# Row maxima sent into lasting score tiles by four small DMAs a step instead of four VectorE scalings, with another order of TensorE's slots

## The chip, the cores and the metric

The kernel runs on one core of a Trainium2 chip. The metric is the device time of one execution in microseconds (us); the median of several runs is compared. The engines are called as the profile calls them: PE is TensorE (PEld its weight loads), DVE is VectorE, ACT is ScalarE, POOL is GpSimd, SP is SyncE, which here only issues DMAs.

## The reference

One transformer block over 2048 tokens of width 1024, with a conditioning vector c that shifts, scales and gates both halves. The attention half treats the tokens as four segments of 512; each of 32 heads (of width 32) takes a causal softmax inside the segment and adds, by a gate of its own, what a linear-attention memory M of all earlier segments gives. The FFN half is gated by GELU. Cut to what matters:

```python
h = _layernorm(x) * (1 + ca) + sa
q, k, v = heads(h @ wq), heads(h @ wk), heads(h @ wv)   # 32 heads, 4 segments of 512
for s in range(4):
    logits = q[s] @ k[s].T * Dh**-0.5 + mask             # causal inside the segment
    a_dot = softmax(logits) @ v[s]
    pq = phi(q[s])                                       # phi(t) = t + 1 if t > 0 else exp(t)
    a_mem = (pq @ M) / (pq @ z + 1e-6)
    o[s] = g * a_mem + (1 - g) * a_dot
    M, z = M + phi(k[s]).T @ v[s], z + phi(k[s]).sum(0)
x = x + ga * (concat(o) @ wo)
h = _layernorm(x) * (1 + cb) + sb
x = x + gb * ((gelu(h @ w_gate) * (h @ w_up)) @ w_down)
```

## The kernel before, in words

**Two parts.** The attention fills about the first 1000 us, the output projection and the FFN the rest. The change touches only the attention. Products keep more than one pass's precision: each operand is split into a high and a low part, and `mm` (L318) issues three matmuls for each of the eight pieces of the contraction (hi x hi, hi x lo, lo x hi): 24 matmuls of 512 columns for each of q, k and v of a step.

**Steps.** `steps` (L1489) lists 32 attention steps. A step is a group g of four heads (j = 0 to 3) in one segment s; segments 0 and 1 go through all eight groups, then segments 2 and 3. Iteration n of the loop runs the scores (`scores`) and the memory (`memory`, `sums`) of step n, the values (`values`) of step n - 1, and the k, v and q products (`kv_part`, `q_part`) of step n + 1.

**Scores twice.** `scores` computes S = q k (L658, row i of 128 queries, head j) to find each row's maximum and sum: DVE adds the mask and takes the negated maximum mm (`sj`, L660), ACT takes the exponential and its row sum ll (L662). `values` computes the transposed scores T = k q again (L722, chunk kc of 128 keys, head j), so that exp(T) (`pt`, L724) can go straight into the product with v (O, L731), after POOL has cut it at the diagonal (L725). The maximum must be subtracted inside the T matmul. For that the tiles ks and qs have 128 rows: rows 0 to 95 hold three pieces of k and q (sent there by DMA, L350 and L378), and rows 96 to 127 hold, in ks, a one-hot pattern of the head (`selj`, written once, L461), and in qs, minus the maximum. Which of these 32 rows carries the maximum of which query block and head is fixed by the pattern `eye`.

**How the maxima reach qs.** The 16 maxima of a partition are split in hi and lo (`mt`, L668 and L669), transposed by DVE in four pieces of 32x32 (`tt`, L673), and then written four times, once for each block i of 128 queries, by a scaling of all 32 rows (L675): row r of tt times `seli[r, i]`, which is one where the row belongs to block i and zero elsewhere. So the rows of other blocks become zero in the same instruction. qs is a fresh tile for each step, two buffers of tag "qs" in turn.

**What frees what.** PSUM has two buffers "mm" (v, k and q products in turn), five "s" (S, T, the transposes vT, kT, R, Y, and the memory's sums) and one "o" (O). A v product's buffer is freed by ACT's copy `vr` (L325); a k product's by `kh`, `kl` and `kn` (L340, L341, L345); a q product's by `qh` (L367), `ql` (L368), and from segment 1 on by `eq` and, last, `pq` (L376).

**Order.** PE's order is written by hand. In each iteration of the loop the string ORDER (ORDER0 in the first) is read letter by letter, and each letter takes the next piece of one generator: V values, S scores, A sums, M memory, K kv_part, Q q_part, N the layernorm of the segments to come, side loads at odd positions. One K piece is two of the eight pieces of a product, 6 matmuls; four K pieces make v, four make k (the transposes vT in the middle of the second), the ninth sends k. In the first eight steps the letter N also brings transposes of the norm. DVE, ACT, POOL and SP are ordered by a scheduler in the loop; in `start()` they too run in the order of the code.

**The start.** `start()` (L415 on) does the layernorm of segments 0 and 1, the conditioning products and step 0's q, k and v. The norm of segment 1 is the generator `norm`; each `next(norm)` does one tile of 128 tokens: statistics on DVE, the inverse root as a power on POOL (L197, `rsa`), a product on DVE (`mra`, L480), the scaling on DVE and ACT (`rx`, L484 and L486).

**Late loads.** `load_late` (L828) puts half of wo into four tiles that the attention no longer uses: two fresh ones of tag "qs" and the two ks tiles.

Of the kernel before, what the change touches and what calls it, by code (L numbers as in the profile page):

```python
# [12 lines left out]
F32R = mybir.dt.float32r  # L13
AF = mybir.ActivationFunctionType
ALU = mybir.AluOpType
# [4 lines left out]
P = 128  # L20
# [9 lines left out]
L = 512  # L30
# [6 lines left out]
def block_kernel(ctx: ExitStack, tc: tile.TileContext, x, c, wmod, wms, wq, wk, wv, wo, beta, wg, wu, wd, out):  # L37
    nc = tc.nc
    f32 = lambda ap: ap.bitcast(F32)
# [45 lines left out]
    def t2(name, tag, bufs=1, dt=F32, shape=(P, L)):  # L85
        return (p1 if tag in ("qs", "row") else pa).tile(list(shape), dt, name=name, tag=tag, bufs=bufs)

    def cs(shape, name, dt=F32, **kw):
        return const.tile(shape, dt, name=name, **kw)
# [10 lines left out]
    ones = cs([P, P], "ones")  # L100
    ident = cs([P, P], "ident")
    mask = pa.tile([P, L], F32, name="mask")
    sel4 = cs([P, 4], "sel4")
    blk = pa.tile([P, P], F32, name="blk")
    selj = cs([P, 4], "selj")
    seli = cs([P, 4], "seli")
    mhalf = cs([P, 4], "mhalf")
    bb = cs([P, H], "bb")
    gall = cs([P, H], "gall")
# [181 lines left out]


    hT, W, Mst, ST, SC, PK = {}, {}, {}, {}, {}, {}
    ks_t = []
    for n in range(2):
        k = p1.tile([P, 4, L], F32R, name=f"ks{n}")
        ks_t.append(k)
# [66 lines left out]
    def q_out(n, s, nm, ps):  # L364
        qh = t2("qh" + nm, "sp", bufs=4, dt=F32R)
        ql = t2("ql" + nm, "sp" if n else "sj", bufs=4 if n else 3, dt=F32R)
        nc.scalar.activation(qh, ps, AF.Copy, scale=SCALE)  # L367
        nc.vector.scalar_tensor_tensor(ql, ps, SCALE, f32(qh), op0=ALU.mult, op1=ALU.subtract)  # L368
        qs = t2("qs" + nm, "qs", bufs=2, dt=F32R, shape=(P, 4, L))
        pq = None  # L370
        if s > 0:
            e = tmp_tile("eq" + nm)
            nc.scalar.activation(e, ps, AF.Exp)
            nc.vector.tensor_scalar_min(e, e, 1.0)
            pq = t2("pq" + nm, "pq", bufs=2)
            nc.vector.scalar_tensor_tensor(pq, ps, 0.0, e, op0=ALU.max, op1=ALU.add)  # L376
        for qd, srct in ((0, qh), (1, ql), (2, qh)):
            nc.sync.dma_start(f32(qs[32 * qd:32 * qd + 32]), f32(srct))  # L378
        state(n)[0], state(n)[3] = qs, pq
# [35 lines left out]
    def start():  # L415
# [20 lines left out]
        def select(dst, src, **kw):  # L436
            nc.gpsimd.affine_select(dst, src, **kw)

        nc.vector.memset(ones, 1.0)
        eye = tmp_tile("eye")[:, :32].rearrange("p (j i l) -> p j i l", j=4, i=4)  # L440
        select(eye, ones[:, :32].rearrange("p (j i l) -> p j i l", j=4, i=4), pattern=[[-8, 4], [-2, 4], [-1, 2]],
               compare_op=ALU.is_equal, fill=0.0, base=-96, channel_multiplier=1)
        select(ident, ones, pattern=[[-1, P]], compare_op=ALU.is_equal, fill=0.0, base=0, channel_multiplier=1)
        pick = tmp_tile("pick")[:, :P].rearrange("p (j d) -> p j d", d=DH)
# [7 lines left out]

        nc.vector.memset(mhalf, -0.5)
        nc.vector.tensor_reduce(selj, eye.rearrange("p j i l -> p j (i l)"), axis=AX.X, op=ALU.add)
        nc.vector.tensor_copy(seli, eye[:, 0, :, 0])
        for j in range(4):
            for part in range(2):
                if j or part:
                    nc.vector.tensor_add(seli, seli, eye[:, j, :, part])
        for k in ks_t:  # L460
            nc.scalar.activation(k[96:128], selj[96:128].unsqueeze(2).to_broadcast([32, 4, L]), AF.Copy)  # L461
            if k is ks_t[0]:
# [152 lines left out]
        low(7)  # L615
        products(6, 7)
        next(norm)
        kk = k_out(0, nm, ps[2])
        k_send(0, *kk)
        q_out(0, 0, nm, ps[0])  # L620
# [26 lines left out]
    def scores(n, g, s):  # L647
# [5 lines left out]
        for i in range(4):  # L653
            nk = max(256, (i + 1) * P)
            nv = (i + 1) * P
            for j in range(4):
                ps = s_ps(f"S{nm}_{j}{i}")
                nc.tensor.matmul(ps[:, :nk], qs[:96, j, i * P:(i + 1) * P], ks[:96, j, :nk], start=True, stop=True)  # L658
                sj = t2(f"sj{nm}_{j}{i}", "sj", bufs=3)
                nc.vector.tensor_tensor_reduce(out=sj[:, :nv], in0=ps[:, :nv], in1=mask[:, L - nv:], scale=-1.0,  # L660
                                               scalar=3.4e38, op0=ALU.add, op1=ALU.min, accum_out=mm[:, j, i:i + 1])
                nc.scalar.activation(sj[:, :nv], sj[:, :nv], AF.Exp, bias=mm[:, j, i:i + 1], scale=-1.0,  # L662
                                     accum_out=ll[:, i, j:j + 1])
            if i < 3:
                yield
# [6 lines left out]
        for a in range(4):  # L672
            nc.vector.transpose(tt[96:128, 32 * a:32 * a + 32], mtf[32 * a:32 * a + 32])  # L673
        for i in range(4):
            nc.vector.tensor_scalar(qs[96:128, :, i * P:(i + 1) * P], tt[96:128].unsqueeze(1).to_broadcast([32, 4, P]),  # L675
                                    seli[96:128, i:i + 1], None, op0=ALU.mult)

        rc = t2("rc" + nm, "rc", bufs=2, shape=(P, 4, 4))
        nc.vector.reciprocal(rc, ll)
# [147 lines left out]

    def load_late():  # L828
        rs = [None] * 5
        for k in range(5):  # L830
            if k < 4:
                rs[k] = fetch(wo[1, k], f"o1_{k}")
            if k > 0:
                w = t2(f"wo1_{k}", "qs", bufs=2, dt=F32R, shape=(P, 4, L)) if k < 3 else ks_t[k - 3]
                wot[1].append(split_w(gated(rs[k - 1], 1), w.rearrange("p (a b) t -> p a (b t)", a=2)))
            yield

# [648 lines left out]


    steps = [(hf, g, s) for hf in range(2) for g in range(G) for s in (2 * hf, 2 * hf + 1)]
    ORDER = "K N K K V K V N K K V V K N V K S Q S V V Q S Q A S K M Q V V"  # L1489
    ORDER0 = "N N N N N N N N K K K K S K S K S K A S K Q Q Q K M Q"  # L1490
    none = iter(())
    todo = []
# [115 lines left out]
```

## Time and profile before

| what | value |
|---|---|
| median of 3 runs | 2776.38 us (2775.57 to 2776.82) |
| the profiled execution's own time | 2777.42 us |
| its span | 2775.6 us |
| mean granted TensorE clock | 0.999 |
| busy share of PE, DVE, ACT, POOL | 98%, 63%, 46%, 20% |
| the 128 scalings into qs (L675) on DVE | 479 ns at least, 481 median, 1035 at most, from 76.8 to 978.4 us |

A row of a timeline gives the start in us, the duration in us (of a group of like instructions, from the first's start to the last's end), the engine, the line, the operation, "out<-in" by the program's names, the tile's shape and the count; in brackets stands how long the engine was idle ahead of it and which instruction it waited for. A row of the waits gives who waited, on whom, the sum in us, the number of times and the longest. A row of the windows gives a stretch of the span, its length, the busy time of PE, PEld, DVE, ACT and POOL in it, the granted clock, and the share and rate of the DMAs.

### The profile page before, as it was taken

To read this page: it belongs to the slowest core of one execution; us is meant where nothing else is said; L and a number is where in the kernel's file an instruction comes from. 1 tells how busy PE (TensorE), PEld (TensorE's weight loads), DVE (VectorE), ACT (ScalarE), POOL (GpSimd) and SP (SyncE) were. 2 spreads that over 40 slices of the span, in tenths; PEclk is the share of its full clock that TensorE was granted. 3 is DMA by queue.
4 is the path that set the end of the run, shared out by engine and by line. 5 is a ranking of instruction groups with operands and counts; after the bars stand their busy time and mean duration, and the time that the engine had idled before them with its cause. 6 is when DMAs were issued, how large, how long until landed. Compare 5 with 4: busy or idle time off the path is not lost.

```text
span 2775.6 us, 38577 instructions
## 1 busy us (share of the span) xinstructions
PE 2729.4 (98%) x13336; PEld 2206.0 (79%) x13336; DVE 1760.7 (63%) x3719; ACT 1287.3 (46%) x2855; POOL 542.0 (20%) x988
## 2 busy tenths in 40 slices
PE   7999999999999999999999999999999999999999
PEld 5777777777777777888888887888888888888887
DVE  7665657767565844777776768667778754434543
ACT  6788767677676735234343324233223243332220
POOL 1333333333332531100000002000000002012442
PEclk9999999999999999999999999999999999999999
DMA  7666656665555648655655644334567595544652
GB/s 258 125 142 152 146 114 129 150 135 126 114 111 96 156 164 252 194 208 208 218 202 195 239 169 167 123 145 143 190 239 254 213 314 177 181 138 156 206 188 80
DMA packets 229604, 480.18 MB, mean 173 GB/s; under 512 B 17440, under 2 KB 92192, under 8 KB 229408
## 3 DMA queue, kind: packets, MB, share of 16 engines
q1 hardware_dynamic: 229408, 477.72, 57.1%
q8 instruction: 105, 1.72, 0.3%
q14 instruction: 91, 0.75, 0.1%
HBM read 300.96 MB, written 126.35 MB: 154 GB/s over the span
## 4 chain that ended last, share of the span: by engine, by line
PE 86%; DVE 6%; issue 2%; ACT 2%; DMA 1%; POOL 1%; SPq 0%; DVEq 0%; ACTq 0%; POOLq 0%
PE f L1286 36%; PE d L1452 19%; PE k L318 6%; PE q L318 5%; PE y L790 5%; PE v L318 3%; PE S L658 3%; PE O L731 3%; PE T L722 3%; DVE qs L675 1%; PE M L638 1%; DVE sj L660 1%; PE R L745 1%; PE num L696 1%; PE vT L334 0%
## 5 line engine op out<-in xcount | busy, mean ns | idle before, releaser
L1286 PE MATMUL f<-A,B 128*128 128x512 f32 x4704 | 1073.2, 390 | 4.4 <-DVE c L1251 2.7
L1286 PEld LDWEIGHTS f<-A,B 128*128 128x128 f32 x4704 | 881.3, 188 | 189.7 <-issue 2.3
L1452 PE MATMUL d<-wb,ah 128*128 128x512 f32 x2352 | 534.3, 389 | 0.2 <-DVE wb L1337 0.2
L1452 PEld LDWEIGHTS d<-wb,ah 128*128 128x128 f32 x2352 | 441.3, 188 | 92.9 <-DVE wb L1337 0.8
L660 DVE CUSTOM_DVE_ANT_0 sj<-S,mask 128x384 f32<-128x384 f32 (+3 forms) x512 | 227.8, 487 | 183.2 <-PE S L658 174.5
L662 ACT ACTIVATE sj<-sj,mm 128x384 f32<-128x384 f32 (+3 forms) x512 | 282.3, 556 | 28.2 <-DVE mm L660 26.0
L724 ACT ACTIVATE pt<-T 128x256 f32<-128x256 f32 (+3 forms) x512 | 184.9, 457 | 119.0 <-PE T L722 113.4
L1337 DVE TENSOR_TENSOR ah<-ar,ah 128x1792 fp32r<-128x1792 f32 x56 | 116.1, 2073 | 187.5 <-ACT ah L1336 187.5
L725 POOL TENSOR_SCALAR_AFFINE_SELECT pt<-pt 128x128 f32<-128x128 f32 x512 | 164.7, 340 | 335.5 <-ACT pt L724 328.3
L1336 ACT ACTIVATE ah<-ar 128x1792 fp32r<-128x1792 f32 x56 | 95.3, 1702 | 284.6 <-PE d L1452 250.6
L1253 ACT ACTIVATE g<-g 128x512 f32<-128x512 f32 x56 | 35.4, 632 | 301.0 <-DVE g L1253 301.0
L160 POOL TENSOR_TENSOR w<-r,w 128x256 fp32r<-128x256 f32 x180 | 132.9, 770 | 165.3 <-ACT w L155 147.7
L924 DVE TENSOR_TENSOR B<-t,B 128x512 fp32r<-128x512 f32 x168 | 116.0, 691 | 56.4 <-ACT B L927 56.3
L1360 POOL TENSOR_TENSOR yo<-u,gbb 128x256 f32<-128x256 f32 x32 | 29.3, 940 | 548.0 <-ACT gbb L132 545.2
L927 ACT ACTIVATE B<-t 128x512 fp32r<-128x512 f32 x168 | 105.4, 628 | 63.7 <-PE f L1286 60.0
L790 PE MATMUL y<-wo,hho 128*128 128x512 f32 x384 | 125.7, 393 | 0.0
L722 PE MATMUL T<-qs,ks 128*128 128x256 f32 (+2 forms) x512 | 115.1, 339 | 7.8 <-DVE ry L704 2.9
L722 PEld LDWEIGHTS T<-qs,ks 128*128 128x128 f32 x512 | 82.9, 188 | 48.9 <-issue 21.7
L1250 ACT ACTIVATE g<-f 128x512 f32<-128x512 f32 x56 | 33.5, 598 | 176.5 <-PE f L1286 176.5
L924 DVE TENSOR_TENSOR B<-rg,B 128x512 fp32r<-128x512 f32 x112 | 77.4, 692 | 52.6 <-ACT B L927 52.4
L658 PE MATMUL S<-ks,qs 96*128 96x256 f32 (+2 forms) x512 | 108.2, 332 | 0.8 <-DVE mm L660 0.8
L1378 POOL TENSOR_TENSOR xo<-xo,yo 128x256 f32<-128x256 f32 x64 | 70.5, 1128 | 194.1 <-DMA xo<-x_d 153.5
(248 smaller groups left out, 4335.9 us busy)
## 6 DMA issues: line engine op xcount, KB each, us to landing
ar<-hid_d SPq DMA_DIRECT2D x56, 896.0 KB, 5.1
rg<-wg SPq DMA_DIRECT2D x56, 512.0 KB, 4.7
ru<-wu SPq DMA_DIRECT2D x56, 512.0 KB, 5.5
hid_d<-g SPq DMA_DIRECT2D x56, 512.0 KB, 3.0
sc<-hid_d SPq DMA_DIRECT2D x56, 512.0 KB, 5.6
hid_d<-sc SPq DMA_DIRECT2D x56, 512.0 KB, 2.9
br<-wT_d SPq DMA_DIRECT2D x49, 512.0 KB, 6.0
ks<-kh SPq DMA_DIRECT2D x64, 256.0 KB, 5.6
```

The lines of the kernel that those rows point to most:

```text
L160: eng.tensor_sub(w[:, 1, k:k + 256], r[:, k:k + 256], f32(w[:, 0, k:k + 256]))
L318: nc.tensor.matmul(ps, w[:, a], b, start=(kt == 0 and a == 0 and b is hi), stop=(kt == KT - 1 and a == 1))
L658: nc.tensor.matmul(ps[:, :nk], qs[:96, j, i * P:(i + 1) * P], ks[:96, j, :nk], start=True, stop=True)
L660: nc.vector.tensor_tensor_reduce(out=sj[:, :nv], in0=ps[:, :nv], in1=mask[:, L - nv:], scale=-1.0, scalar=3.4e38, op0=ALU.add, op1=ALU.min ...
L662: nc.scalar.activation(sj[:, :nv], sj[:, :nv], AF.Exp, bias=mm[:, j, i:i + 1], scale=-1.0, accum_out=ll[:, i, j:j + 1])
L722: nc.tensor.matmul(ps[:, :nn], ks[:, j, kc * P:(kc + 1) * P], qs[:, j, L - nn:], start=True, stop=True)
L724: nc.scalar.activation(pt, ps[:, nn - n:nn], AF.Exp)
L725: nc.gpsimd.affine_select(pt[:, :P], pt[:, :P], pattern=[[1, P]], compare_op=ALU.is_ge, fill=0.0, base=0, channel_multiplier=-1)
L790: nc.tensor.matmul(ps, b[:, i * P:(i + 1) * P], w[:, a, g % 2], start=(g == 0 and a == 0 and b is hi), stop=(g == G - 1 and a == 1))
L924: eng.tensor_sub(dst[:, k], a[:, k], b[:, k])
L1286: nc.tensor.matmul(ps, B[m, i][:, a, kt * P:(kt + 1) * P], A[p, i, kt][b], start=(start and kt == 0 and a == 0 and b == 0), stop=(kt == 3 ...
L1452: nc.tensor.matmul(ps[t], ops[n][:, x, k, t * P:(t + 1) * P], b[:, y, kk % 2], start=(kk == 0 and x == 0 and y == 0), stop=(kk == 13 and x ...
```

## The change: the maxima are sent by DMA

The four scalings go. mm and mt are laid out by block first, then head, and the pattern `eye` with them, so that the eight rows of one block i (four heads, hi and lo) stand together: rows 96 + 8i to 103 + 8i. Four DMAs a step, issued by SP, copy these eight rows of tt to the same eight rows of qs, at the columns of block i, for each of the four heads (8 x 4 x 128 numbers, 16 KB). The other rows are no longer written: there are two lasting qs tiles, `qs_t`, used in turn, whose rows 96 to 127 are set to zero once in `start()` by eight POOL operations (the mask minus itself). `seli` and its eight DVE instructions go. `load_late` begins two pieces later and uses qs_t. The string ORDER has its letters in another order.

```diff
@@ start: the pattern, seli
-        select(eye, ..., pattern=[[-8, 4], [-2, 4], [-1, 2]],
+        select(eye, ..., pattern=[[-2, 4], [-8, 4], [-1, 2]],
-        nc.vector.tensor_copy(seli, eye[:, 0, :, 0])
-        for j in range(4):
-            for part in range(2):
-                if j or part:
-                    nc.vector.tensor_add(seli, seli, eye[:, j, :, part])
@@ start, behind the second next(norm)
+        for n in range(2):
+            q = t2(f"qs{n}", "qs", bufs=2, dt=F32R, shape=(P, 4, L))
+            qs_t.append(q)
+            for j in range(4):
+                nc.gpsimd.tensor_tensor(q[96:128, j], mask[96:128], mask[96:128], op=ALU.subtract)
@@ q_out
-        qs = t2("qs" + nm, "qs", bufs=2, dt=F32R, shape=(P, 4, L))
+        qs = qs_t[n % 2]
@@ scores
-                                               ..., accum_out=mm[:, j, i:i + 1])
+                                               ..., accum_out=mm[:, i, j:j + 1])
         for i in range(4):
-            nc.vector.tensor_scalar(qs[96:128, :, i * P:(i + 1) * P], tt[96:128].unsqueeze(1).to_broadcast([32, 4, P]),
-                                    seli[96:128, i:i + 1], None, op0=ALU.mult)
+            own = slice(96 + 8 * i, 104 + 8 * i)
+            nc.sync.dma_start(f32(qs[own, :, i * P:(i + 1) * P]), tt[own].unsqueeze(1).to_broadcast([8, 4, P]))
@@ load_late
+        yield
+        yield
-                w = t2(f"wo1_{k}", "qs", bufs=2, dt=F32R, shape=(P, 4, L)) if k < 3 else ks_t[k - 3]
+                w = (qs_t[0], ks_t[0], qs_t[1], ks_t[1])[k - 1]
@@ the order of an iteration
-    ORDER = "K N K K V K V N K K V V K N V K S Q S V V Q S Q A S K M Q V V"
+    ORDER = "K N K K K K V K V K N V V K V N S Q S V V Q S Q A S K M Q V V"
```

The first V of an iteration, T0 (the four T matmuls of chunk 0), stood behind three K pieces and stands behind five; the last T group, T3, stood two letters ahead of the first S with a K piece between them, and the new string has no K piece there. Where k comes, in the iteration that computes the values of group 3 in segment 2 (T_2) and k and v of group 4, PE had, from the last v pieces on:

```order
L318 MATMUL v_2_9091<-hhh_3_1_6020,w_1_4_8858 128x512
L722 MATMUL T_2_00_9112<-qs_2_8714,ks_111 128x512
L722 MATMUL T_2_10_9117<-qs_2_8714,ks_111 128x512
L722 MATMUL T_2_20_9122<-qs_2_8714,ks_111 128x512
L722 MATMUL T_2_30_9127<-qs_2_8714,ks_111 128x512
L318 MATMUL v_2_9091<-hhh_4_0_6068,w_1_4_8858 128x512
```

and has now:

```order
L317 MATMUL v_2_9068<-hhh_4_1_6071,w_1_4_8846 128x512
L317 MATMUL k_2_9098<-hhh_1_0_5793,w_1_4_8921 128x512
L317 MATMUL k_2_9098<-hlh_1_0_5794,w_1_4_8921 128x512
L317 MATMUL k_2_9098<-hhh_1_0_5793,w_1_4_8921 128x512
L317 MATMUL k_2_9098<-hhh_1_1_5825,w_1_4_8921 128x512
L317 MATMUL k_2_9098<-hlh_1_1_5826,w_1_4_8921 128x512
L317 MATMUL k_2_9098<-hhh_1_1_5825,w_1_4_8921 128x512
L721 MATMUL T_2_00_9112<-qs_494,ks_110 128x512
```

So all of v and the first piece of k now stand ahead of T0. On ACT, at the end of the same values, where pt_2_j3 is the exp of T3 for head j and kh the high part of the k just finished, the order was:

```order
L724 ACTIVATE pt_2_32_9212<-T_2_32_9210 128x256
L724 ACTIVATE pt_2_03_9223<-T_2_03_9221 128x128
L724 ACTIVATE pt_2_13_9228<-T_2_13_9226 128x128
L724 ACTIVATE pt_2_23_9233<-T_2_23_9231 128x128
L724 ACTIVATE pt_2_33_9238<-T_2_33_9236 128x128
L340 ACTIVATE kh_2_9247<-k_2_9168 128x512
```

and is now:

```order
L723 ACTIVATE pt_2_32_9195<-T_2_32_9193 128x256
L339 ACTIVATE kh_2_9204<-k_2_9098 128x512
L723 ACTIVATE pt_2_03_9212<-T_2_03_9210 128x128
L723 ACTIVATE pt_2_13_9217<-T_2_13_9215 128x128
L723 ACTIVATE pt_2_23_9222<-T_2_23_9220 128x128
L723 ACTIVATE pt_2_33_9227<-T_2_33_9225 128x128
```

kh has moved from behind the four exps of T3 to ahead of them. On DVE, behind the transposes tt of that step, the scheduler's order was (qs are the scalings, wm a product of the conditioning that is spread over the loop):

```order
L673 STREAM_TRANSPOSE tt_2_9029<-mt_2_9026 32x32 x4
L701 RECIPROCAL dn_2_9057<-dn_2_9057 128x16
L675 TENSOR_SCALAR qs_2_8714<-tt_2_9029,seli 32x4x128 x4
L679 RECIPROCAL rc_2_9038<-ll_2_8895 128x16
L702 TENSOR_TENSOR dn_2_9057<-dn_2_9057,gall 128x16
L368 SCALAR_TENSOR_TENSOR ql_3_9072<-q_3_8916,qh_3_9071 128x512
L680 TENSOR_TENSOR rc_2_9038<-rc_2_9038,omg 128x16
L704 TENSOR_TENSOR ry_2_9058<-num_2_0_9051,dn_2_9057 128x256
L374 TENSOR_SCALAR eq_3_9076<-eq_3_9076 128x512
L753 TENSOR_TENSOR R_3_8959<-R_3_8959,Y_3_9084 128x512
L376 SCALAR_TENSOR_TENSOR pq_3_9079<-q_3_8916,eq_3_9076 128x512
L146 ISA wm_8957,modT<-wm_8957,scb 128x1024
```

and is now:

```order
L672 STREAM_TRANSPOSE tt_2_9007<-mt_2_9004 32x32 x4
L700 RECIPROCAL dn_2_9035<-dn_2_9035 128x16
L678 RECIPROCAL rc_2_9016<-ll_2_8873 128x16
L701 TENSOR_TENSOR dn_2_9035<-dn_2_9035,gall 128x16
L752 TENSOR_TENSOR R_3_8937<-R_3_8937,Y_3_9061 128x512
L679 TENSOR_TENSOR rc_2_9016<-rc_2_9016,omg 128x16
L703 TENSOR_TENSOR ry_2_9036<-num_2_0_9029,dn_2_9035 128x256
L367 SCALAR_TENSOR_TENSOR ql_3_9050<-q_3_8894,qh_3_9049 128x512
L145 ISA wm_8935,modT<-wm_8935,scb 128x1024
L373 TENSOR_SCALAR eq_3_9053<-eq_3_9053 128x512
L375 SCALAR_TENSOR_TENSOR pq_3_9056<-q_3_8894,eq_3_9053 128x512
```

The scalings are gone, and wm has moved from behind pq to ahead of it.

More of the change, by code (lines that the diff above doesn't have):

```diff
@@ L105, in block_kernel @@
     selj = cs([P, 4], "selj")
-    seli = cs([P, 4], "seli")
     mhalf = cs([P, 4], "mhalf")
@@ L293, in block_kernel @@
     hT, W, Mst, ST, SC, PK = {}, {}, {}, {}, {}, {}
-    ks_t = []
+    ks_t, qs_t = [], []
     for n in range(2):
@@ L440, in start @@
         eye = tmp_tile("eye")[:, :32].rearrange("p (j i l) -> p j i l", j=4, i=4)
-        select(eye, ones[:, :32].rearrange("p (j i l) -> p j i l", j=4, i=4), pattern=[[-8, 4], [-2, 4], [-1, 2]],
+        select(eye, ones[:, :32].rearrange("p (j i l) -> p j i l", j=4, i=4), pattern=[[-2, 4], [-8, 4], [-1, 2]],
                compare_op=ALU.is_equal, fill=0.0, base=-96, channel_multiplier=1)
@@ L660, in scores @@
                 nc.vector.tensor_tensor_reduce(out=sj[:, :nv], in0=ps[:, :nv], in1=mask[:, L - nv:], scale=-1.0,
-                                               scalar=3.4e38, op0=ALU.add, op1=ALU.min, accum_out=mm[:, j, i:i + 1])
-                nc.scalar.activation(sj[:, :nv], sj[:, :nv], AF.Exp, bias=mm[:, j, i:i + 1], scale=-1.0,
+                                               scalar=3.4e38, op0=ALU.add, op1=ALU.min, accum_out=mm[:, i, j:j + 1])
+                nc.scalar.activation(sj[:, :nv], sj[:, :nv], AF.Exp, bias=mm[:, i, j:j + 1], scale=-1.0,
                                      accum_out=ll[:, i, j:j + 1])
```

## The prediction, as put on record

> **What bounds the kernel now.** I read the page's busy table and the windows first, then what PE (TensorE) waited for, then PE, DVE and ACT over two steps of the attention, then the start. The change touches the start and the 32 attention steps (to about 1000 us); the FFN behind them is the same program. The windows (length, busy us of PE, PEld, DVE, ACT, POOL) of the first and the last of the five stretches of attention that I took from 69 to 1000 us:
>
> ```profile
> PE 2729.4 (98%) x13336; PEld 2206.0 (79%) x13336; DVE 1760.7 (63%) x3719; ACT 1287.3 (46%) x2855; POOL 542.0 (20%) x988
> ...
> 69.00:200.00 131.00, 128.60 (x743) 102.41 (x742) 81.69 (x282) 103.43 (x283) 46.84 (x108) 1.00 0.63 135
> ...
> 800.00:1000.00 200.00, 194.69 (x1098) 149.04 (x1097) 135.39 (x420) 132.95 (x372) 87.07 (x172) 1.00 0.56 128
> ```
>
> PE is the bound: idle 2.4 of 131 us and 5.3 of 200, 18.2 us in all five. DVE has a third of its time free there (135 of 200 us busy), so DVE work that goes is worth only the PE waits that it causes. Those waits, by releaser (us in total, times, longest):
>
> ```profile
> PE k L318 <- ACT vr L325: 3.3, 7, 0.5
> PE T L722 <- DVE ry L704: 2.9, 5, 0.9
> PE T L722 <- DVE qs L675: 2.6, 4, 0.8
> PE k L318 <- DVE pq L376: 0.7, 2, 0.3
> ```
>
> Together 9.5 us. A busy PE hides a part of its waits inside modelled durations, so I also measured, step by step, the stretch on PE from the first v matmul to the first O matmul. It holds the same matmuls in every step from 344 us on. The first of those 21 stretches, two in the middle with their stall, and the last:
>
> ```profile
> 344.28 0.39 PE L318 MATMUL v<-hha,w 128*128 128x512 f32 x1
> ...
> 354.63 0.64 PE L731 MATMUL O<-pt,vx 128*32 128x512 f32 x4
> ...
> 714.68 0.48 PE L318 MATMUL v<-hhh,w 128*128 128x512 f32 x1
> ...
> 720.42 0.89 PE L722 MATMUL T<-qs,ks 128*128 128x512 f32 x2 [0.90 <-DVE ry L704]
> ...
> 726.54 1.71 PE L731 MATMUL O<-pt,vx 128*32 128x512 f32 x16
> ...
> 743.76 0.48 PE L318 MATMUL v<-hhh,w 128*128 128x512 f32 x1
> ...
> 751.55 0.50 PE L318 MATMUL k<-hhh,w 128*128 128x512 f32 x1 [0.46 <-ACT vr L325]
> ...
> 754.95 1.39 PE L731 MATMUL O<-pt,vx 128*32 128x512 f32 x12
> ...
> 916.98 0.47 PE L318 MATMUL v<-hhh,w 128*128 128x512 f32 x1
> ...
> 927.96 0.64 PE L731 MATMUL O<-pt,vx 128*32 128x512 f32 x4
> ```
>
> They last 10.35, 11.86, 11.19 and 10.98 us. Over the 21 the mean is 11.30, some 0.9 above the unobstructed first; I take 0.8 for each of the 29 steps of this form, 23 us that PE loses in this stretch. That is all that the removal can win inside the loop; 9.5 (what the waits name) is its more cautious reading.
>
> **The removed scalings.** DVE in the step of 714 us and, for two rows, in the next step; then the 128 scalings as one group:
>
> ```profile
> 713.48 0.69 DVE L660 CUSTOM_DVE_ANT_0 sj<-S,mask 128x512 f32<-128x512 f32 x1
> ...
> 714.81 0.86 DVE L673 STREAM_TRANSPOSE tt<-mt 32x32 f32<-32x32 f32 x4
> ...
> 715.99 2.72 DVE L675 TENSOR_SCALAR qs<-tt,seli 32x512 fp32r<-32x512 f32 x4
> ...
> 721.55 0.69 DVE L376 SCALAR_TENSOR_TENSOR pq<-q,eq 128x512 f32<-128x512 f32 x1
> 722.15 1.22 DVE L146 CUSTOM_DVE_ANT_0 wm<-wm,scb 128x1024 f32<-128x1024 f32 x1
> ...
> 751.00 0.68 DVE L376 SCALAR_TENSOR_TENSOR pq<-q,eq 128x512 f32<-128x512 f32 x1
> ...
> L675 DVE TENSOR_SCALAR qs<-tt,seli x128: 479/481/1035, 76.8 to 978.4; 32x512 fp32r<-32x512 f32 x128
> ```
>
> Four scalings are 4 x 0.481 = 1.92 us a step, 2.72 in the step shown. All that stands behind them on DVE (rc, ry, ql, eq, pq) comes that much earlier, and T, now two K slots later, no longer meets ry: the 23 us go. But the new order asks for something that the old one did not. A K slot is 6 matmuls; at the 0.227 us from start to start that v shows in this trace it is 1.37 us. The k accumulation now starts right behind the 24 v matmuls, at 714.68 + 5.46 = 720.1, and it needs the PSUM buffer "mm" of the q before it, which pq, its last reader, frees. pq ended at 722.24; without the scalings at 719.5, and with wm (1.22), which the new DVE order puts ahead of it, at 720.7: k waits 0.6. In the next step pq ended at 751.68, so 749.8 without the scalings, against k wanted at 743.76 + 5.46 = 749.2: 0.6 again. Some steps have no wm; I take 0.5 x 29 = 14 us lost (0 to 23). Net of the removal: 23 - 14 = **-9 us** (-16 to 0).
>
> **T3 directly ahead of S.** The new string has no K slot between the last T group and the first S group of the next step. ACT and PE at that place before:
>
> ```profile
> 728.66 1.21 ACT L724 ACTIVATE pt<-T 128x256 f32<-128x256 f32 x4 [3.59 <-PE T L722]
> 730.52 0.79 ACT L724 ACTIVATE pt<-T 128x128 f32<-128x128 f32 x4 [0.64 <-PE T L722]
> 732.20 0.60 ACT L340 ACTIVATE kh<-k 128x512 fp32r<-128x512 f32 x1 [0.90 <-PE k L318]
> ...
> 730.14 0.64 PE L722 MATMUL T<-qs,ks 128*128 128x256 f32 x4
> ...
> 732.00 0.64 PE L658 MATMUL S<-ks,qs 96*128 96x256 f32 x4
> ```
>
> T and S share five PSUM buffers in rotation, so S_1 to S_3 take the buffers of T3_0 to T3_2 and wait for their exps. Before, T3 started at 730.14, its exps ran from 730.52 to 731.31, and S came at 732.00: no wait. After, ACT has kh ahead of the four exps. kh can start when the last k matmul, just ahead of T3, has drained, at about +0.2 us; it takes 0.5 to 0.6; the exps follow at +0.8 in steps of 0.2, so the third ends at about +1.4. PE would like S_3 at about +0.9 and gets it at about +1.4. I take 0.45 us x 21 steps, and 0.2 for the 8 early steps, where norm's transposes stand between: 9.5 + 1.6 = **+11 us** (3, if kh starts at once or lies in the shadow of PE's own latency, to 16). Nothing hides it: PE has only S next.
>
> **The zeroed rows at the start.** Eight POOL operations of 32x512 are put between two of the norm's powers on POOL:
>
> ```profile
> 44.31 0.55 POOL L197 TENSOR_TENSOR rsa<-rsa,mhalf 128x1 f32<-128x1 f32 x1 [1.36 <-DVE rsa L196]
> 49.08 0.59 POOL L197 TENSOR_TENSOR rsa<-rsa,mhalf 128x1 f32<-128x1 f32 x1 [4.22 <-DVE mra L480]
> ...
> 51.41 0.59 POOL L197 TENSOR_TENSOR rsa<-rsa,mhalf 128x1 f32<-128x1 f32 x1 [1.65 <-DVE mra L480]
> ...
> 52.04 0.23 DVE mra L480
> ...
> L183 POOL TENSOR_TENSOR hlh<-rh,hhh 128x512 fp32r<-128x512 f32 x8 | 10.4, 1306 | 8.5 <-DVE hhh L182 8.5
> ...
> L160 POOL TENSOR_TENSOR w<-r,w 128x256 fp32r<-128x256 f32 x180 | 132.9, 770 | 165.3 <-ACT w L155 147.7 <-PE S L658 17.7
> ```
>
> The nearest row by width, 512 columns, is 1306 ns: 8 x 1.31 = 10.4 us from 44.9, done at 55.3. The next power then runs at 55.3 and the last at about 56.1 to 56.7, and mra, which stood at 52.04 on the chain that reaches the first v and S matmuls, starts at 56.7: **+4.7 us**. By the row of 256 columns it is 8 x 0.77 = 6.2, done at 51.1, and the last power hardly moves: about 0.5. If the gaps that the powers had are worth nothing and both transposes slip, 9. I take 4.7 since the width is the same; fewer partitions need not make it shorter. The Trainium skill, GPSIMD Engine Reference, section 3.1 (Elementwise — side-by-side cycle accounting), has about 2.6 cycles an element for such a two-input operation; at 1.2 GHz an estimate by it is 1.1 us, 8.9 for the eight, and the sum would be 1.5 us lower. The eight small DVE operations that made seli at the start stand where DVE waits for ACT anyway: 0. The later loads of wo end beside projections on a busy PE: 0.
>
> **The four transfers.** Does T0 wait for them? SyncE and DMA rows:
>
> ```profile
> L378 SPq DMA_DIRECT2D qs<-qh x64: 547/575/708, 46.1 to 952.1; - x64
> ...
> 719.98 0.55 SPq L378 DMA_DIRECT2D qs<-ql  x1
> 720.57 0.60 SPq L378 DMA_DIRECT2D qs<-qh  x1
> ...
> qs<-qh SPq DMA_DIRECT2D x64, 256.0 KB, 5.2
> ccol<-c SPq DMA_DIRECT2D x1, 4.0 KB, 1.8
> ```
>
> tt ends at 714.81 + 0.86 = 715.67; four issues at 0.575 reach 718.0. One 16 KB transfer lands between 1.8 us (4 KB) and 5.2 us (256 KB) after its issue; by size it is nearer to the 4 KB row, so 2.5: 720.5. T0 is wanted behind 30 matmuls, at 714.68 + 6.83 = 721.5. In the next step tt ends at about 744.2, landing is 749.0, and T0 is wanted at 750.6. It is hidden by 1.0 and 1.6 us of v and k matmuls: **0**. On SyncE the four stand ahead of the next q's sends and the store of R; S needs those q rows over 10 us later, and nobody reads the store soon: 0.
>
> **The sum.** -9 + 11 + 4.7 = +6.7 on the profiled execution's own 2777.42 us, 2784.1. That execution lay 1.04 us over the median of 2776.38, so **2783 us** (2783.1).
>
> **The rivals.**
> (A) Faster: kh is out of the way or S's wait hides, and POOL's zeroing costs about 0.5. For it: before, ACT shows 0.64 and 0.90 us of idle around these exps. Against: the ACT order puts kh first, and the exps cannot start before it. 2777.42 - 9 + 0.5 - 1.04 = 2768; with k's wait gone as well, down to 2755.
> (B) Slower on the other side of the cover: a transfer lands like the 256 KB ones, 5.2 us after the last issue, at 723.2 against 721.5, and 751.7 against 750.6. The wait of 0.5 on pq lies inside, so about 0.9 x 29 = 26 is added: 2809. It decides from a landing of 3.5 us on.
> (C) The gaps only change places: the named 9.5 us of waits go, S costs its low end of 3 and kept pq waits 2, POOL about 4: 2776. PE's 98% speaks for it.
> (D) The four do not overlap in flight: (0.575 + 1.8) x 4 = 9.5 us, landed at 725.3, 3.8 late, less 0.5, about 2.9 in the mean of both steps, x 29 = 84: 2867. The rows above speak against it: the issue at 720.57 follows that of 719.98 by 0.59 us, long before a 4.2 us landing could be over. The Trainium skill, DMA: Bandwidth & Descriptors, section Rules for kernel authors, speaks against this change: transfers under 64 KB are mostly overhead and should be made one; its Anatomy of one DMA has some 2.0 us fixed for each. The 1.8 us of the 4 KB row agrees with that; whether four pay it side by side no row here shows.
>
> **How the numbers follow.** Chances: my forecast 0.42, A 0.26, B 0.12, C 0.16, D 0.04. This kernel's runs agree to 0.05%, and about 0.2% (5.6 us) can be told from no change: faster is under 2770.8, slower over 2781.9. The forecast with its terms' bounds gives 0.26 slower, 0.15 same, 0.01 faster; A 0.24 faster, 0.02 same; B and D 0.16 slower; C 0.12 same and 0.02 on either side. Faster 0.27, same 0.29, slower 0.44. The range leaves out D, two thirds of B and the far end of A: 2762 to 2801. The forecast alone has 2772 to 2794.
>
> **What would show it.** Right, if PE's waits after have k on DVE pq (about 0.5 us, most steps) and S on ACT pt (about 0.45), no T on the transfers, and if the last power at the start comes near 56 us. Wrong, if S's wait on pt is under 0.2 us a step or POOL's eight take under 7 us (then A), or if T waits for a transfer (B, D).

## The result, and the profile after

| | before | changed kernel |
|---|---|---|
| median | 2776.6 us (2775.57 to 2777.76, 4 runs) | 2805.48 us (2803.08 to 2809.06, 4 runs) |
| ratio | | 1.0103, 95% interval 1.0091 to 1.0116 |
| span of the profiled execution | 2775.6 us | 2801.4 us |
| PE busy | 2729.4 us | 2735.9 us |
| DVE busy | 1760.7 us | 1701.5 us |

The kernel became 28.9 us slower (the two profiled executions, 2777.42 and 2803.08 us, differ by 25.7). The forecast was 2783 us: the right sign, a quarter of the size, and 4.5 us outside its range. DVE has 59 us less to do, as the removal of the 128 scalings says. PE, which is the bound, waits more. The windows of the changed kernel that answer to those shown of before (length, busy us of PE, PEld, DVE, ACT, POOL, granted clock, DMA share, GB/s):

```profile
69.00:200.00 131.00, 128.04 (x739) 102.06 (x739) 73.16 (x261) 101.53 (x283) 43.18 (x104) 1.00 0.59 123
...
800.00:1000.00 200.00, 192.62 (x1099) 148.94 (x1098) 117.91 (x401) 137.07 (x389) 73.95 (x164) 1.00 0.61 125
```

PE is idle 3.0 of 131 us (2.4 before) and 7.4 of 200 (5.3 before), and a part of a wait lies hidden in the modelled durations. What PE waited for in the attention is another list than before (us in total, times, longest):

```profile
PE k L317 <- DVE pq L375: 15.7, 15, 2.4
...
PE S L657 <- ACT pt L723: 5.8, 22, 0.3
PE k L317 <- DVE rsa L195: 5.8, 3, 2.2
```

T on ry and on qs, and k on vr, are gone; k on pq and S on pt are new. No T waits for a transfer. (rsa is the DVE instruction nearest in time; the wait in the program is the same one on pq.)

To see the whole wait and not only its idle part, I took PE's starts in the attention, matmul by matmul, and summed by tile how far each start lies behind the closest spacing of a matmul of that shape. This sum is called "by spacing" below; where the closest spacing is set moves a figure by some 2 us, and the difference of two kernels by less. By it k loses 27.7 us (7.7 before), S 21.7 (3.7), T 19.7 (32.6), O 61.9 (65.7; its closest spacing is one of four matmuls side by side, so only the difference counts). k and S cost 38 us more, T and O 17 less, and R, q and the memory's product num 6 more.

**Where k waits.** In the changed kernel, the step that answers to the one at 743.76 us before; PE's first v, first k and T0, then DVE between tt and pq:

```profile
766.15 0.48 PE L317 MATMUL v<-hhh,w 128*128 128x512 f32 x1
...
773.34 0.50 PE L317 MATMUL k<-hhh,w 128*128 128x512 f32 x1 [1.46 <-DVE pq L375]
...
774.84 1.07 PE L721 MATMUL T<-qs,ks 128*128 128x512 f32 x4
```

```profile
765.66 0.86 DVE L672 STREAM_TRANSPOSE tt<-mt 32x32 f32<-32x32 f32 x4
...
769.22 0.68 DVE L367 SCALAR_TENSOR_TENSOR ql<-q,qh 128x512 fp32r<-128x512 f32 x1
769.81 1.39 DVE L145 CUSTOM_DVE_ANT_0 wm<-wm,scb 128x1024 f32<-128x1024 f32 x1
...
771.14 0.95 DVE L373 TENSOR_SCALAR eq<-eq 128x512 f32<-128x512 f32 x1
772.01 0.69 DVE L691 TENSOR_SCALAR mz<-sel,Mt 128x4 f32<-128x4 f32 x1
772.61 0.68 DVE L375 SCALAR_TENSOR_TENSOR pq<-q,eq 128x512 f32<-128x512 f32 x1
```

k is wanted at 766.15 + 5.46 = 771.6, pq ends at 773.3, and k starts with it: 1.7 us lost. ql, wm, eq and mz, all in DVE's one queue, run in front of pq. T0 follows the six k matmuls with no wait: the transfers landed in time.

Which iterations wait shows from k's start behind the first v, 5.46 us where nothing holds it. In the even iterations from 2 to 14 k does not wait: the q whose buffer it takes is then one of segment 0, which has no pq. In the odd ones from 3 to 15 k comes about 2 us late (0.6 in iteration 13), 13.7 us in all. In the 15 from 16 on it comes 0 to 2.4 us late, 13.2 us in all. DVE in iteration 7, one of the odd ones, where k was wanted at 266.5 and started at 269.00:

```profile
265.49 0.68 DVE L190 BATCH_NORM_STATS2 sta<-na 128x6 f32<-128x512 f32 x1
266.87 0.75 DVE L373 TENSOR_SCALAR eq<-eq 128x512 f32<-128x512 f32 x1 [0.69 <-ACT eq L372]
...
268.27 0.68 DVE L375 SCALAR_TENSOR_TENSOR pq<-q,eq 128x512 f32<-128x512 f32 x1
```

**Where S waits.** The last T group and the first S group, on PE, and ACT beside them:

```profile
753.27 0.64 PE L721 MATMUL T<-qs,ks 128*128 128x256 f32 x4
753.75 0.28 PE L657 MATMUL S<-ks,qs 96*128 96x256 f32 x1
754.29 0.73 PE L657 MATMUL S<-ks,qs 96*128 96x256 f32 x3 [0.27 <-ACT pt L723]
754.86 0.39 PE L317 MATMUL q<-hhh,w 128*128 128x512 f32 x1
```

```profile
753.47 0.60 ACT L339 ACTIVATE kh<-k 128x512 fp32r<-128x512 f32 x1 [0.47 <-PE k L317]
753.97 0.78 ACT L723 ACTIVATE pt<-T 128x128 f32<-128x128 f32 x4
```

kh starts 0.2 us after T3, the exps run behind it from +0.70 to +1.48, and the S group takes 1.11 us to the next q matmul, against 0.48 before (732.00 to 732.48):

```profile
732.48 0.40 PE L318 MATMUL q<-hhh,w 128*128 128x512 f32 x1
```

**At the start**, POOL's eight operations, the powers behind them, and the S matmuls of before and of the changed kernel by first and last start:

```profile
44.67 8.46 POOL L616 TENSOR_TENSOR qs<-mask 32x512 fp32r<-32x512 f32 x8
53.21 0.55 POOL L196 TENSOR_TENSOR rsa<-rsa,mhalf 128x1 f32<-128x1 f32 x1
...
53.84 0.78 POOL L196 TENSOR_TENSOR rsa<-rsa,mhalf 128x1 f32<-128x1 f32 x1
```

```profile
L657 PE MATMUL S<-ks,qs x512: 278/337/802, 67.4 to 998.9; 96*128 96x256 f32 x85, 96*128 96x384 f32 x43, 96*128 96x512 f32 x43
```

```profile
L658 PE MATMUL S<-ks,qs x512: 279/334/796, 64.8 to 971.0; 96*128 96x256 f32 x85, 96*128 96x384 f32 x43, 96*128 96x512 f32 x43
```

The last of the powers runs at 53.84 us (51.41 before). The first S is 2.6 us late, the last 27.9. Behind the attention the changed kernel loses nothing more: at the end it is 25.8 us behind.

### The profile page after: what moved, and what is told of

Read it like the earlier page. It is cut to its first block, busy times and chain, and to the rows that moved or that the text cites. A ratio compares the mean times of both kernels' runs of the same rounds, so it can differ in the third digit from the quotient of the medians.

```text
span 2801.4 us, 38601 instructions
## 1 busy us (share of the span) xinstructions
PE 2735.9 (98%) x13336; PEld 2212.7 (79%) x13336; DVE 1701.5 (61%) x3583; ACT 1292.5 (46%) x2855; POOL 538.3 (19%) x996
## 4 chain that ended last, share of the span: by engine, by line
PE 83%; DVE 7%; ACT 3%; issue 3%; DMA 1%; POOL 1%; DVEq 0%; SPq 0%; ACTq 0%; POOLq 0%
PE f L1287 36%; PE d L1453 19%; PE k L317 6%; PE y L789 5%; PE q L317 4%; PE T L721 3%; PE O L730 3%; PE S L657 2%; PE v L317 2%; DVE sj L659 1%; ACT sj L661 1%; PE M L637 1%; PE R L744 1%; DVE wm L145 1%; DMA r<-wq 1%
## 5 line engine op out<-in xcount | busy, mean ns | idle before, releaser
L724 POOL TENSOR_SCALAR_AFFINE_SELECT pt<-pt 128x128 f32<-128x128 f32 x512 | 147.1, 302 | 328.0 <-ACT pt L723 321.0
L657 PE MATMUL S<-ks,qs 96*128 96x256 f32 (+2 forms) x512 | 119.5, 346 | 8.2 <-ACT pt L723 5.8
L340 DVE TENSOR_TENSOR kl<-k,kh 128x512 fp32r<-128x512 f32 x32 | 22.1, 691 | 163.5 <-ACT kh L339 163.5
L657 PEld LDWEIGHTS S<-ks,qs 96*128 96x128 f32 x512 | 88.3, 189 | 27.2 <-ACT pt L723 12.0
L721 PE MATMUL T<-qs,ks 128*128 128x256 f32 (+2 forms) x512 | 109.1, 334 | 0.0
```

Source lines behind the costliest of these rows:

```text
L721: nc.tensor.matmul(ps[:, :nn], ks[:, j, kc * P:(kc + 1) * P], qs[:, j, L - nn:], start=True, stop=True)
L724: nc.gpsimd.affine_select(pt[:, :P], pt[:, :P], pattern=[[1, P]], compare_op=ALU.is_ge, fill=0.0, base=0, channel_multiplier=-1)
```

## The experiments

All ratios are to the kernel before, with its runs on the same chip. Letters of ORDER that were moved are named.

**e1: the transfers with the old string.**

```diff
-    ORDER = "K N K K K K V K V K N V V K V N S Q S V V Q S Q A S K M Q V V"
+    ORDER = "K N K K V K V N K K V V K N V K S Q S V V Q S Q A S K M Q V V"
```

> The changed kernel with the string ORDER of before; the four transfers stay. Theory W (the lost time is two new waits that the new order makes: k on pq, some 27 us in all, and S on the exps of T3, some 18 us): both go, but T0 is wanted two K pieces earlier, 4.7 to 5.1 us after the last sj of a step, where the last of the four issues ends at about 4.5 us. If a transfer lands 1.8 us after its issue, T0 waits about 1.4 us a step for DMA: 2790 to 2810 us, with PE's waits naming the transfers under T. Theory D (the transfers land at once and the time went to the order alone): 2760 to 2770, no wait of T on DMA. Theory E (the time went to neither but to the start and to DVE's new order): about 2805, with k still waiting on pq.

Measured 2817.93 us, ratio 1.0150 (1.0135 to 1.0165). Theory W holds in its mechanism, above its range. The waits of PE, then PE's T0 of one step, SP's four issues and the transposes ahead of them on DVE:

```profile
PE T L721 <- DMA qs<-tt: 28.9, 23, 3.8
```

```profile
753.27 0.48 PE L317 MATMUL v<-hhh,w 128*128 128x512 f32 x1
...
758.79 1.16 PE L721 MATMUL T<-qs,ks 128*128 128x512 f32 x4 [1.16 <-DVE eq L373]
```

```profile
754.28 2.97 SPq L675 DMA_DIRECT2D qs<-tt  x4
```

```profile
753.39 0.86 DVE L672 STREAM_TRANSPOSE tt<-mt 32x32 f32<-32x32 f32 x4
```

tt ends at 754.25, the fourth issue at 757.25, and T0 starts at 758.79 (the row names eq, which only ended last; the program has T0 wait for the four transfers). In nearly all steps T0 starts 4.5 us behind tt, whichever of the two segments it is: 3.0 us of issues and 1.5 behind the end of the last. That is 6.0 us behind the last sj in the late steps, close to the 6.3 that the theory took. T0 loses 45 us by spacing, 1.9 a step in the first half, where every second tt comes later behind its sj, and 1.05 in the second. What lies above the range is mostly that the other matmuls of T lose some 9 us more than in the changed kernel. Four scalings took 2.0 us for the same. k does not wait here (0.8 us by spacing): both new waits are the new string's.

**e2: the new string with the scalings kept.**

```diff
-    ORDER = "K N K K V K V N K K V V K N V K S Q S V V Q S Q A S K M Q V V"
+    ORDER = "K N K K K K V K V K N V V K V N S Q S V V Q S Q A S K M Q V V"
```

> The kernel before with only the new string ORDER; the four scalings on DVE stay and no transfer is added. Theory W: k waits on pq and S on the exps of T3 as in the changed kernel, and pq comes another 1.9 us later a step, behind the scalings: 2805 plus up to 29 x 1.9 us, so 2825 to 2860. Theory D': if the waits come with the transfers (SP's queue, landing) rather than with the order: 2770 to 2780.

load_late was left as it was, so that a part of wo is loaded over a qs tile whose T matmuls still follow; this kernel's output is not the reference's. Measured 2833.38 us, ratio 1.0206 (1.0188 to 1.0224). k loses 48.9 us by spacing and S 20.5:

```profile
PE k L318 <- ACT vr L325: 23.6, 15, 4.3
PE k L318 <- DVE pq L376: 9.1, 7, 1.9
```

So the new string without the transfers makes k and S wait as well, and without the scalings the same string is 28 us faster. But pq is only a part of k's wait here. In iteration 18, for instance, k starts at 612.46, with the end of vr on ACT (611.80 + 0.60), while pq ends at 613.99: k cannot have q's buffer there, and the only other "mm" buffer is v's, which vr frees. In the late iterations of this kind k waits for that copy alone (0.69 us each). In the early ones (3.7 us in iteration 3) vr stands on ACT behind eq, which starts as ql ends on DVE, and ql stands behind the scalings. So the 28 us contain another assignment of the two buffers too, and are a rough value of the removal; in e13 every late k starts with the end of pq, as in the changed kernel.

**e3: a Q piece between T3 and S.**

```diff
-    ... V N S Q S V V Q S Q A S K M Q V V
+    ... V N Q S V S V Q S Q A S K M Q V V
```

> The changed kernel with the first Q piece put between T3 and the first S group (one S group then stands behind it as well, ahead of O): six q matmuls, 1.4 us, cover the exps of T3. Theory W: the wait of S on pt goes, some 18 us: 2783 to 2792, k on pq unchanged. Rival (what S does not wait there it waits later, for pq or for the next exps): over 2800.

Measured 2795.11 us, ratio 1.0070 (1.0055 to 1.0085): 10 us off, less than theory W's range. No S waits for pt any more; by spacing S inside its groups loses 8.7 us in place of 18, and the later groups, now closer together, keep that rest. The wait was real, its price 10 and not 18 in this place.

**e4: T0 directly behind v, ahead of the first k piece.**

```diff
-    K N K K K K V K V K N ...
+    K N K K K V K K V K N ...
```

> The changed kernel with T0 directly behind v, ahead of the first k piece. T0 is wanted 6.0 to 6.5 us after the last sj. Theory W: k is wanted 0.9 us later, so its wait on pq shrinks from about 27 us to about 9; T0 waits for a transfer by 0 to 0.5 us a step, 0 to 15 us: 2787 to 2805, and the wait of T on DMA tells when the transfers land. Rival (T0's cover was ample): 2785 with no wait on DMA at all.

Measured 2791.81 us, ratio 1.0053 (1.0036 to 1.0069): 14 us off. k loses 5.0 us by spacing (27.7 before this edit), T waits for the transfers by 5.5 us in 4 steps and about 11 us in all ahead of T0. T0 waits in every second step of the first half (0.9 to 2.4 us); in the second half it starts 6.1 or 6.6 us behind the last sj, where the transfers need 6.0, and does not wait.

**e5: q's PSUM buffer freed by ACT.**

```diff
-            nc.vector.scalar_tensor_tensor(pq, ps, 0.0, e, op0=ALU.max, op1=ALU.add)
+            nc.scalar.activation(pq, ps, AF.Relu)
+            nc.vector.tensor_add(pq, pq, e)
```

> The changed kernel, but the q product's PSUM buffer is freed earlier: ACT writes max(q, 0) into pq's tile, and DVE adds the exponential to it from SBUF, so that pq no longer reads PSUM. One ACT operation of 128x512 a step more, 0.6 us, on an engine that is busy under 0.75 of these stretches. Theory W (k waits because pq, the last reader of q's buffer, comes late on DVE): k's wait of some 27 us goes, less 0 to 8 us for the added ACT work: 2778 to 2788. Rival (pq is only named as the last, ql or the sending of k hold k as well; or the wait moves to the next link): 2795 to 2806.

Measured 2789.84 us, ratio 1.0049 (1.0034 to 1.0064): 15.6 us off, 2 us short of theory W's range, with the order of PE as it was. The wait of k is all but gone:

```profile
PE k L317 <- ACT pq L375: 1.5, 3, 0.8
```

By spacing k loses 3.8 us, 24 less; T loses 6 more, probably behind ACT's added work. That k waited for pq as the last reader of q's buffer is shown.

**e7: the zeroing behind the norm's last power.** The eight operations move from between two next(norm) to behind the loop over norm.

> The changed kernel with the eight POOL operations that zero the tiles put behind the last power of the norm at the start. Theory W: the first scores come as in the kernel before, 2.6 us earlier; of that 1.4 to 2.6 us stay: 2802 to 2804. Rival (the start has nothing to do with it): 2805.5.

Measured 2802.93 us, ratio 1.0099 (1.0084 to 1.0114). The first S comes at 66.0 us, 1.4 earlier; the time is 2.5 us off, which the intervals do not tell from nothing.

**e8: e3 and e4 together.**

> The changed kernel with both moves of the string that were tried singly: T0 directly behind v (2791.8 by itself) and the first Q piece ahead of the first S group (2795.1 by itself). If the two waits are independent, their gains of 13.7 and 10.4 us add up: 2781. If one wait only takes the place of the other: about 2791.

Measured 2794.52 us, ratio 1.0067 (1.0052 to 1.0082): no better than either alone. With the Q piece earlier and v earlier, T0 stands closer to the last sj than the transfers allow:

```profile
PE T L721 <- DMA qs<-tt: 8.8, 7, 2.7
PE T L721 <- DVE modT L145: 6.2, 3, 5.4
```

**e6: e3, e5 and e7 together.**

> The changed kernel with the Q piece ahead of S, the early freeing of q's buffer by ACT, and the zeroing behind the norm; T0 stays behind the first k piece. Theory W: the waits of k (27 us) and S (10 us as measured) and 2 us at the start go, and 0 to 8 us of ACT work come: 2766 to 2775, the transfers hidden, so that the removal of the scalings shows as a gain against the kernel before. Rival (the waits of PE in this stretch are one chain that only moves): over 2785.

Measured 2792.11 us, ratio 1.0051 (1.0035 to 1.0068). The gains did not add up: k waits for ACT's share of pq again (6.9 us in 3 steps), T for the transfers (2.2 us), S inside its groups 13.6 us by spacing. In both runs that join e3 with another mending, e8 and this one, the gain of e3 does not add to it.

**e9: wm later.**

```diff
-                    todo.append((pos + 14, lambda got=got: mod_col(*got[0], behind=True)))
+                    todo.append((pos + 20, lambda got=got: mod_col(*got[0], behind=True)))
```

> The changed kernel with the product wm of the conditioning (1.22 us on DVE, one or two a step) emitted six letters later, so that it stands behind pq on DVE and in DVE's idle stretch. Theory W (k waits on pq, and pq is late because of what the new DVE order puts ahead of it): in the twelve steps in which wm ran ahead of pq, pq comes up to 1.2 us earlier and k waits up to that less: 6 to 12 us off, 2794 to 2800. Rival (wm is in no one's way, another operation takes its place ahead of pq): 2804 to 2807.

Measured 2800.25 us, ratio 1.0082 (1.0067 to 1.0097): 5 us off, at the edge of what the intervals tell apart. By spacing k loses 21.2 in place of 27.7. wm was a part of the queue ahead of pq, not most of it.

**e10: A, the memory's sums, between T3 and S.**

```diff
-    ... V N S Q S V V Q S Q A S K M Q V V
+    ... V N A S Q S V V Q S Q S K M Q V V
```

> The changed kernel with the letter A (the eight matmuls of the memory, 1.06 us, in the steps of the segments 0 to 2) moved from the third S group to between T3 and the first S group. Theory W: it covers the exps of T3 in 23 of the 31 iterations, where S waited some 0.5 us more than before: 8 to 12 us off, 2793 to 2798. Rival (A was the cover of the last S group, whose wait for a PSUM buffer now grows by as much): 2803 to 2808.

Measured 2787.87 us, ratio 1.0040 (1.0025 to 1.0055): 17.6 us off, more than expected. k's wait shrank as well (18.8 us by spacing), and 7.7 us of the gain lie in the four iterations 13 to 16 alone, of which more stands under "The sum" below. The kernel is its own control, since A is empty in the steps of the last segment. First an iteration with the sums M between T3 and S, then the next one without:

```profile
711.43 0.64 PE L721 MATMUL T<-qs,ks 128*128 128x256 f32 x4
711.90 1.06 PE L637 MATMUL M<-vx,pk 128*128 128x130 f32 x8
712.72 0.72 PE L657 MATMUL S<-ks,qs 96*128 96x256 f32 x4
...
739.36 0.64 PE L721 MATMUL T<-qs,ks 128*128 128x256 f32 x4
739.83 0.28 PE L657 MATMUL S<-ks,qs 96*128 96x256 f32 x1
740.37 0.73 PE L657 MATMUL S<-ks,qs 96*128 96x256 f32 x3 [0.27 <-ACT pt L723]
```

With M the four S run through in 0.72 us; without it the second comes 0.54 us behind the first.

**e11: e10, e5 and e7 together.**

> The changed kernel with A ahead of S, q's buffer freed early by ACT, and the zeroing behind the norm. If the gains of 15.6 (by itself), 8 to 12 and 2.5 us add up: 2775 to 2780, level with the kernel before or a little faster. If A and ACT's added work get in each other's way, as the Q piece did: 2786 to 2792.

Measured 2779.14 us, ratio 1.0010 (1.0001 to 1.0020): 26.3 us of the 28.9 are back. The gains add up here. k loses 2.7 us by spacing, S 10.0; the transfers stay, hidden but for 1.8 us.

**e12: e10, e9 and e7 together.**

> The changed kernel with A ahead of S, wm behind pq, and the zeroing behind the norm; ACT has no added work. Adding up: 2805.5 - 8 to 12 - 6 to 12 - 2.5 = 2779 to 2789. If the waits only change places: over 2792.

Measured 2786.67 us, ratio 1.0038 (1.0025 to 1.0051): e10 with little added. The range held it, but wm behind pq brought nothing here that the intervals show. From last sj to last sj the trace tells two effects apart: iterations 17 to 29 take 4.7 us less than in e10, and 13 to 16 take 7.1 us more.

**e13: e11 with the scalings in place of the transfers.** seli, the fresh qs tiles and the four scalings are those of before; string, load_late and the freeing by ACT are those of e11.

> The kernel before with its four scalings, but with all else that the combined kernel (2779.1 us) has: the changed string with A ahead of S, the later loads of wo, and q's buffer freed early by ACT. The difference to that kernel is the value of the removal at an equal order. Theory F (the forecast's term: the removal is worth 20 us or more wherever the order is not the limit): 2799 to 2810. Theory W (DVE's work counts only where its end frees what PE waits for, and that is gone with q's buffer freed by ACT, except ql, which now ends 1.9 us later, about when k is wanted): 2780 to 2790.

Measured 2830.61 us, ratio 1.0198 (1.0184 to 1.0212): 51.5 us slower than e11. It lies beyond both expectations, on the side of theory F; W fell. PE's waits, then DVE, ACT and PE in one step:

```profile
PE k L318 <- ACT pq L376: 31.5, 19, 4.4
```

```profile
764.52 2.17 DVE L676 TENSOR_SCALAR qs<-tt,seli 32x512 fp32r<-32x512 f32 x4
...
767.25 0.68 DVE L368 SCALAR_TENSOR_TENSOR ql<-q,qh 128x512 fp32r<-128x512 f32 x1
```

```profile
767.96 0.60 ACT L373 ACTIVATE eq<-q 128x512 f32<-128x512 f32 x1 [2.43 <-DVE ql L368]
768.45 0.62 ACT L683 ACTIVATE rx<-rc 128x512 f32<-128x512 f32 x1
768.97 0.59 ACT L376 ACTIVATE pq<-q 128x512 f32<-128x512 f32 x1
```

```profile
769.61 0.50 PE L318 MATMUL k<-hhh,w 128*128 128x512 f32 x1 [0.72 <-ACT pq L376]
```

ACT's freeing of q's buffer hangs on DVE after all: on ACT it stands behind rx and eq, ACT is idle for 2.43 us until eq starts as ql ends on DVE (767.93), and ql stands on DVE behind the scalings. k starts with the end of ACT's pq. So with k directly behind v, the 1.9 us of scalings a step lie on k's path. From last sj to last sj 30 of the 51.5 us lie in the iterations up to the 12th. Not all of the 51.5 us are the scalings themselves: TensorE's granted clock was lower in this run too (last section).

**e14: e11 and e9 together.**

> The combined kernel (A ahead of S, q's buffer freed early by ACT, zeroing behind the norm) with wm behind pq as well. If wm was in the way only of pq, which no longer frees what k waits for: 2778 to 2780, no gain. If it delays ql or ry too: 2774 to 2777, as fast as the kernel before.

Measured 2786.75 us, ratio 1.0034 (1.0022 to 1.0047): 7.6 us slower than e11, which neither case had. S loses 15.5 us by spacing in place of 10.0, waiting for DVE's readers of its buffers (5.7 us named). All of these named waits lie between 483 and 520 us, where DVE splits the next segments' h between the sj; from last sj to last sj iterations 13 to 16 take 7.7 us more than in e11, those up to the 12th 2.9 less. wm runs in none of these places. So the loss came with where the scheduler then put the splitting, and not with wm standing in the way.

**e15: the kernel before with q's buffer freed by ACT.**

> The kernel before with nothing changed but q's buffer freed early by ACT. Its k waits on pq for 0.7 us in all, so theory W expects no gain, and a loss where ACT's 0.6 us a step delays the exps: 2775 to 2783. Were the freeing of q's buffer worth something apart from the new order, it would be 2765 to 2772.

Measured 2777.11 us, ratio 0.9999 (0.9990 to 1.0008). In the old order nobody waits for that buffer, and freeing it early is worth nothing.

## Why the prediction was wrong in size, point by point

**The removed scalings.** That they were worth some 23 us of waits holds: T, O and the old waits of k lose 24 us less by spacing. **The step that failed is "I take 0.5 x 29 = 14 us lost (0 to 23)"** for k on pq: it measured 27.7 us by spacing, 24 of which e5 took away. The mechanism and the place were right; the size was read from two late steps and multiplied by all. Of the 29, seven do not wait, since segment 0's q has no pq. Seven early ones wait about 2 us, since the norm's statistics and the wait for ACT's eq stand ahead of pq on DVE too, and the 15 late ones 0.9 us on average in place of 0.5. In the step shown wm, eq and mz took longer than in the rows of before (eq 0.95 us where another step had 0.42). The second of the two rows was no evidence for this wait either: in the kernel before, k started at 751.55 while pq ended at 751.68, so it did not hold q's buffer there, and its row names vr. The two buffers are not strictly in turn in that kernel (six late iterations are like this one); in the changed kernel no k starts before the pq ahead of it ends. So the net of this part was about +4, not -9.

**T3 ahead of S.** The mechanism was right as written, kh ahead of the exps included (0.63 us more for the S group in the step shown, 0.45 taken). The size was low: 18 us more by spacing, where the forecast had 11. Some 2.6 of the 18 are no wait for an exp but lie in the one iteration under "The sum". What e10 gets back, 17.6 us, is not a measure of it alone, as said there.

**The start.** +4.7 forecast, 2.6 found at the first S; the last power ran at 53.84, not 56.1. POOL's operation took 1038 ns, not the 1306 of the row with 128 partitions; the estimate of 1.1 us by the Trainium skill (GPSIMD Engine Reference, section 3.1) was nearer. In e7, at another time, the same operation took 1221 ns at the median. e7 got 1.4 us back at the first S.

**The transfers.** "Hidden: 0" holds in the changed kernel. From the end of tt to T0 it took 4.5 us in e1, where 2.3 + 2.5 = 4.8 were forecast. The total was near by two errors that cancel: an issue took 0.716 us at the median, not 0.575, so four took 3.0, and the last one landed 1.5 us behind its issue's end, not 2.5. Rival B did not occur, though the time came near its price. Rival D is excluded for the transfers: four that each pay 1.8 us in turn behind an issue of 0.7 would need 10 us, and e1 shows 4.5. The 2.0 us that the prediction takes from the Trainium skill (DMA: Bandwidth & Descriptors, Anatomy of one DMA) stand in that section for transfers that GpSimd issues, and these are issued by SyncE. The rule of the Trainium skill (DMA: Bandwidth & Descriptors, Rules for kernel authors) that transfers under 64 KB are mostly overhead agrees with e1, where 64 KB in four transfers took 3.0 us of issues and 1.5 us of landing. Whether one larger transfer would be quicker was not tried.

**The sum.** Against the forecast k is 13 us more, S 7 more and the start 2 less, and R, q and num add 6 that the forecast did not have. These are sums by spacing; with -1 for the scalings they make 30 us where 28.9 were measured. Some 5 us of them lie in one iteration, the 15th to the 16th step, 34.4 us from last sj to last sj against 29.0 before: S loses 3.7 us there (0.1 before) and k 2.8 (0.9). S waits there twice for DVE, at 525.2 and 526.6, and not for an exp:

```profile
PE S L657 <- DVE mm L659: 2.1, 2, 1.2
```

```profile
520.00:530.00 10.00, 7.46 (x32) 5.31 (x31) 10.00 (x27) 4.84 (x15) 4.76 (x4) 0.87 0.68 130
530.00:540.00 10.00, 10.00 (x40) 8.41 (x40) 7.98 (x29) 4.56 (x12) 0.35 (x1) 0.79 0.29 73
```

DVE is busy for all 10 us there, with the splitting of the next segments' h between the sj. Why the scheduler bunched it there was not tried by itself, but it moves the time of several runs. The four iterations 13 to 16 take 115.4 us before, 123.3 in the changed kernel, 115.6 in e10, 115.5 in e11, 122.7 in e12 and 123.2 in e14. So nearly 8 us of what e10 and e11 gain come from these four iterations, and the part of this that is not k's and S's usual wait has no experiment of its own.

**Why the change did not win.** In the old order the scalings cost no more than the 24 us above, as v and T stood ahead of k; the transfers need 4.5 us where the scalings took 2.0, so T0 came late (e1, +41 us). The new string hides the transfers, but asks for k at once, and so puts DVE's queue on the path. Under that string the removal is worth 28 us (e2) or 51 us (e13 against e11), and with its two waits mended it comes back to the time of before and, in the runs made, no further. In e11 the iterations 17 to 29 take 367.8 us against 371.4 before, 3.6 us less by one profile of each; the iterations up to the 12th take 3.7 us more and give it back.

## What to carry to other kernels

An edit that moves work to a slower but free path (here from DVE to DMA) is priced by its latency, and by what the order must give up to hide that latency. When an order is changed, go through every buffer that the moved instruction needs and find its last reader, in more than two steps and in each phase of the program: a queue of small operations ahead of that reader is not the same in all of them. And a gain under the new order is no gain until it is held against the old order. Where two runs differ by a few us, compare them iteration by iteration: in e12 and e14 a place that the edit did not touch hid its effect.

## What was not expected of the hardware

- An issue of a 16 KB transfer (8 x 4 x 128) took SP 0.716 us at the median, against 0.60 for one of 256 KB beside it, so that four hold SP for 3.0 us:

```profile
L675 SPq DMA_DIRECT2D qs<-tt x128: 677/716/1017, 79.4 to 1005.8; - x128
...
L377 SPq DMA_DIRECT2D qs<-qh x64: 547/601/627, 45.8 to 980.1; - x64
```

- TensorE's granted clock fell to 0.87 and 0.79 in two windows of 10 us (above) in which PE was idle by at most 1.2 us at a time, 2.5 us in all. In finer windows it is one stretch at half clock:

```profile
527.40:534.20 6.80, 6.38 (x21) 4.96 (x21) 6.54 (x26) 4.52 (x13) 1.32 (x2) 0.50 0.28 40
```

No window of 10 us between 60 and 1200 us of the kernel before lay under 0.995. In e13 there are six such stretches in the attention, of 3.4 or 6.8 us and 30.7 us together; the first, from 150.1 us, begins at the end of a wait of k of 3.05 us. Half a clock costs at most half of such a stretch: an estimate of 3.4 us for the changed kernel's profiled execution and 15 for e13's. The mean clock of the executions was 0.994 to 0.997 in the changed kernel, 0.997 to 0.999 in e11 and 0.991 to 0.993 in e13, against 0.997 to 0.999 before, so a part of the larger differences above may go with the clock and not with the waits alone. Why it fell at these waits and not at others as long (k's 2.44 us at 504.66) was not tried.
